# A transformer block on one core: shared exponentials and a new queue order in attention, and PSUM copies on ACT one tile ahead in the output projection

## The chip, the core and the metric

The kernel runs on one core of a Trainium2 chip. The metric is the device time in microseconds (us), lower is better. A core has a matmul engine (PE, TensorE; its weight loads are shown as PEld), a vector engine (DVE), an activation engine (ACT), a general engine (POOL) and a queue processor (SP) that starts DMAs. In these kernels each engine works through its own queue of instructions and waits for the others at semaphores. Every matmul here writes to PSUM, which the kernels use as eight banks of 512 float32 columns, and DVE or ACT takes the results from there, mostly to SBUF.

## The reference

One pre-norm block, batch 1, 2048 tokens, width 1024, bfloat16:

```python
h  = x + A(layernorm(x))      # 32 heads of 32, four segments of 512 tokens
h2 = h + B(layernorm(h))      # SwiGLU, hidden width 3584
# A, for every head and segment s:
p = softmax(q_s @ k_s.T * scale + causal_mask)
o = g * (phi(q_s) @ M) / (phi(q_s) @ z) + (1 - g) * (p @ v_s)   # memory read
M, z = M + phi(k_s).T @ v_s, z + phi(k_s).sum()                 # memory update
# phi(t) = t + 1 where t > 0, exp(t) elsewhere; then o @ wo
```

## The kernel before

The stages follow one another: LN1 with the Q, K, V projections, attention, the output projection with LN2, the feed-forward network (FFN). Attention works on groups `g` of four heads. One segment of one group has four score blocks `kc` (128 keys each; the causal mask leaves 512, 384, 256 and 128 queries). A block's scores for the four heads lie in PSUM banks 0 to 3, and one exp takes all four to SBUF. Because there is one such set of banks, the next block's score matmuls wait for that exp. The triangle on the diagonal is masked afterwards by a multiplication on DVE.

The loop runs the head of segment c together with the tail of the segment before it:

```python
for g in range(NG):                    # 8 groups
    for s in range(NSEG):              # 4 segments
        c = seg_begin(g, s)
        head_kc(c, 0)                  # score matmuls, exp on ACT, mask on DVE
        if prev is not None:
            tail_u_tile(prev, 0)       # exp(scores) @ V, query tile 0; the first
            tail_u_tile(prev, 1)       #   of these waits for the last combine
        head_kc(c, 1)
        if prev is not None:
            tail_u_tile(prev, 2)
        head_kc(c, 2)
        if prev is not None:
            tail_u_tile(prev, 3)
            tail_T(prev)               # transposes of phi(K), copied by DVE
        head_kc(c, 3)
        if prev is not None:
            tail_rest(prev)            # memory read (PE), memory update matmuls (PE),
                                       # combine (DVE: reciprocal, product, sum),
                                       # memory update (DVE: 1 + 8 small operations)
        if s == 1 and g + 1 < NG:
            group_prep(g + 1)          # phi(K), phi(Q) of the next group:
        prev = c                       #   DVE min, ACT exp, DVE max and add; twice
```

The output stage, for 16 tiles of 128 tokens (cut to its order):

```python
t_otT(0); mmA(0)
for t in range(1, NT):
    t_otT(t)        # PE transposes the attention output into banks 0, 1;
                    # DVE copies one half to SBUF, ACT the other
    hadd_ln(t - 1)  # DVE: residual add, LN2 statistics, square root on ACT, apply: hn
    mmA(t)          # 16 matmuls, wait for both copies of t_otT(t)
    ...
    hnT_tr(t - 1)   # PE transposes hn; ACT copies one half, DVE the other
```

The softmax here doesn't subtract the row's maximum and nothing guards it: scores larger than these inputs give would overflow.

## Time and profile before

The median is 1248.84 us of 4 runs (1247.97 to 1251.16). The stage boundaries below are the first transposes of the attention output and the first load of FFN weights.

| stage | from, to (us) | length |
|---|---|---|
| LN1, Q, K, V | 0 to 217 | 217 |
| attention | 217 to 542.9 | 325.9 |
| output projection, LN2 | 542.9 to 642.7 | 99.8 |
| FFN | 642.7 to 1247.2 | 604.5 |

The windows table of the kernel before, for attention and the output stage; its columns are stretch, length, busy time with count for PE, PEld, DVE, ACT and POOL, granted PE clock (1 is full speed), DMA share and GB/s:

```profile
217.00:542.86 325.86, 136.04 (x2656) 82.06 (x2657) 204.08 (x490) 183.34 (x145) 0.00 (x0) 0.51 0.02 8
542.86:642.66 99.80, 77.45 (x512) 39.30 (x512) 69.41 (x144) 25.09 (x49) 0.00 (x0) 0.96 0.15 43
```

Of the 325.9 us of attention, PE is busy 136, DVE 204 and ACT 183. With no engine near full, it is the order of waits that sets the time. The Trainium skill, "Perfetto Trace Analysis", Roofline, says that where matmul and HBM utilization are both low the kernel is bound by latency, that is by stalls and dependencies. The 8 GB/s and 42% PE in this row agree. The granted clock is 0.51.

The timeline of ACT over one group (kernel before; start, length, engine, line, operation, and in brackets the idle time before it with what ended it) shows the rhythm. Line 589 is the exp of a score block, line 552 an exp of the preparation:

```profile
329.17 1.88 ACT L589 ACTIVATE eTbuf<-psall 128x2048 bf16<-128x2048 f32 x1
...
336.62 1.88 ACT L589 ACTIVATE eTbuf<-psall 128x2048 bf16<-128x2048 f32 x1 [0.98 <-PE psall L580]
...
344.63 1.88 ACT L589 ACTIVATE eTbuf<-psall 128x2048 bf16<-128x2048 f32 x1 [0.98 <-PE psall L580]
...
352.39 1.88 ACT L589 ACTIVATE eTbuf<-psall 128x2048 bf16<-128x2048 f32 x1 [0.72 <-PE psall L580]
355.64 1.45 ACT L589 ACTIVATE eTbuf<-psall 128x1536 bf16<-128x1536 f32 x1 [1.38 <-PE psall L580]
357.60 1.02 ACT L589 ACTIVATE eTbuf<-psall 128x1024 bf16<-128x1024 f32 x1 [0.51 <-PE psall L580]
359.03 0.60 ACT L589 ACTIVATE eTbuf<-psall 128x512 bf16<-128x512 f32 x1 [0.40 <-PE psall L580]
363.64 1.48 ACT L552 ACTIVATE tmp<-tmp 128x1536 bf16<-128x1536 bf16 x1 [4.01 <-DVE tmp L548]
367.54 1.48 ACT L552 ACTIVATE tmp<-tmp 128x1536 bf16<-128x1536 bf16 x1 [2.42 <-DVE tmp L548]
369.11 1.88 ACT L589 ACTIVATE eTbuf<-psall 128x2048 bf16<-128x2048 f32 x1
```

The large exps (2048 elements per partition) start 7.45, 8.01, 7.76 and 16.72 us apart: 39.9 us per group. The long one contains the preparation. There the next large exp stands in ACT's queue behind two preparation exps that wait for DVE.

The chain of waits (kernel before; start, length, what) shows why an ordinary segment takes 8 us with 4.95 us of exps:

```profile
344.27 0.37 DVE rrs L709
344.66 1.24 DVE prod L712
345.92 0.70 DVE onat L718
...
346.67 0.52 PE psall L625 x12
347.19 0.47 PE psall L580 x4
347.68 1.46 ACT eTbuf L589
```

The combine (lines 709, 712 and 718) must end before the first twelve attention x V matmuls (line 625) may write to its banks, and the score matmuls of block 1 (line 580) stand behind those in PE's queue. Two groups from the page of the kernel before, the attention x V matmuls and the output projection (line, engine, operation, operands, shapes, count, then busy us and mean ns of one, then the idle time before them and what ended it):

```profile
L625 PE MATMUL psall<-vaug,eTbuf 128*128 128x33 bf16 x1280 | 53.5, 193 | 55.4 <-DVE onat L718 50.1
L849 PE MATMUL psall<-wosb,otT 128*128 128x512 bf16 x256 | 59.4, 386 | 16.0 <-ACT otT L833 16.0
```

PE waits 50.1 us for the combine in attention, and in the output stage 16.0 us for ACT's copy. The timeline of one tile there (kernel before):

```profile
580.04 3.61 PE L849 MATMUL psall<-wosb,otT 128*128 128x512 bf16 x16 [1.02 <-ACT otT L833]
583.08 0.55 DVE L883 TENSOR_SCALAR hn<-hnat,ln2mv,ln2rstd 128x1024 bf16<-128x1024 bf16 x1
583.68 0.62 PE L896 MATMUL psall<-ident,hn 128*128 128x128 bf16 x8
584.14 0.61 PE L819 MATMUL psall<-ident,onat 128*128 128x128 bf16 x8
585.77 3.61 PE L849 MATMUL psall<-wosb,otT 128*128 128x512 bf16 x16 [1.02 <-ACT otT L833]
```

The projection's matmuls (line 849) start 5.73 us apart (580.04, 585.77), with 1.02 us of PE idle in each tile. Line 883 applies LN2 and gives hn, line 896 is its transposes, line 819 those of the attention output.

### The profile page before, as it was taken

The numbers are of one execution on the slowest core, as the hardware profiler recorded it, in microseconds if no ns is written. First come the engines' busy times: TensorE is split into PE (matmuls) and PEld (weight loads), VectorE is DVE, ScalarE is ACT, GpSimd is POOL, SyncE is SP. The second block draws the span as 40 slices with busy tenths as digits, with TensorE's granted clock in tenths as the row PEclk, the third lists the DMA queues.
The fourth block names the chain that finished last, engine by engine and source line by source line (L and its number), as shares of the span: only waits on it lengthen the run. The fifth ranks groups of instructions, "written<-read, shape, count | busy, mean of one in ns | idle before, by whom it ended". The sixth has DMA issues, their size and how long they took to land.

```text
span 1247.2 us, 16150 instructions
## 1 busy us (share of the span) xinstructions
PE 984.3 (79%) x6752; PEld 470.6 (38%) x6752; DVE 506.8 (41%) x1010; ACT 339.9 (27%) x423; POOL 21.0 (2%) x43
## 2 busy tenths in 40 slices
PE   4988988254334443567859999999999997999997
PEld 2444444132222222334424444444444443444443
DVE  5240310466666665657744333333333331011011
ACT  3224123565555655622221111111111110000000
POOL 1000000000000000000000000000000000011011
PEclk9989999555555555579979999999999998999999
DMA  8000000100000000011121111111211102455453
GB/s 303 1 34 1 1 1 7 62 2 1 1 1 1 1 1 1 1 35 43 51 76 34 35 34 35 34 34 34 63 40 35 34 1 101 142 196 176 161 178 126
DMA packets 54232, 66.05 MB, mean 53 GB/s; under 512 B 1936, under 2 KB 30608, under 8 KB 54160
## 3 DMA queue, kind: packets, MB, share of 16 engines
q1 hardware_dynamic: 52624, 60.83, 15.7%
q0 software_dynamic: 1536, 4.20, 0.9%
q8 instruction: 53, 0.87, 0.3%
q14 instruction: 19, 0.16, 0.0%
HBM read 60.83 MB, written 4.19 MB: 52 GB/s over the span
## 4 chain that ended last, share of the span: by engine, by line
PE 68%; DVE 14%; ACT 14%; issue 2%; DMA 1%; POOL 0%; DVEq 0%; SPq 0%; ACTq 0%; POOLq 0%
PE psall L986 16%; PE psall L992 16%; PE psall L1073 15%; PE psall L383 12%; ACT eTbuf L589 8%; PE psall L849 4%; PE psall L580 3%; DVE prod L712 2%; ACT tmp L552 2%; DVE eTbuf L597 2%; ACT xnT L352 1%; DVE lnst L317 1%; DVE onat L718 1%; DVE pkTg L555 1%; PE psall L625 1%
## 5 line engine op out<-in xcount | busy, mean ns | idle before, releaser
L986 PE MATMUL psall<-hnT,w1b 128*128 128x512 bf16 x896 | 213.3, 381 | 6.6 <-DMA w3b<-in_B_w_dram 6.6
L992 PE MATMUL psall<-hnT,w3b 128*128 128x512 bf16 x896 | 212.8, 381 | 0.0
L1073 PE MATMUL psall<-w2b,hmT 128*128 128x512 bf16 x896 | 196.0, 382 | 7.0 <-DMA w2b<-in_B_w_dram 7.0
L589 ACT ACTIVATE eTbuf<-psall 128x2048 bf16<-128x2048 f32 (+3 forms) x128 | 158.3, 1237 | 84.8 <-PE psall L580 84.1
L1008 DVE TENSOR_TENSOR sg<-sg,psall 128x512 bf16<-128x512 bf16 x112 | 77.0, 688 | 239.7 <-PE psall L992 239.7
L580 PE MATMUL psall<-qT,kT 32*128 32x256 bf16 (+3 forms) x512 | 57.7, 441 | 125.8 <-ACT eTbuf L589 117.9
L1003 ACT ACTIVATE sg<-psall 128x512 bf16<-128x512 f32 x112 | 66.9, 597 | 316.8 <-PE psall L986 316.7
L1073 PEld LDWEIGHTS psall<-w2b,hmT 128*128 128x128 bf16 x896 | 88.1, 98 | 114.8 <-issue 10.8
L986 PEld LDWEIGHTS psall<-hnT,w1b 128*128 128x128 bf16 x896 | 87.9, 98 | 113.3 <-issue 8.6
L992 PEld LDWEIGHTS psall<-hnT,w3b 128*128 128x128 bf16 x896 | 88.0, 98 | 106.9 <-issue 2.2
L625 PE MATMUL psall<-vaug,eTbuf 128*128 128x33 bf16 x1280 | 53.5, 193 | 55.4 <-DVE onat L718 50.1
L1095 DVE TENSOR_TENSOR ob<-hnat,psall 128x512 bf16<-128x512 bf16 x32 | 22.0, 688 | 180.3 <-PE psall L1073 179.9
L597 DVE TENSOR_TENSOR eTbuf<-eTbuf,triu 128x512 bf16<-128x512 bf16 x128 | 54.4, 425 | 81.5 <-ACT eTbuf L589 76.6
L1013 DVE TENSOR_TENSOR hmT<-sg,psall 128x512 bf16<-128x512 bf16 x112 | 76.9, 686 | 3.9
L625 PEld LDWEIGHTS psall<-vaug,eTbuf 128*128 128x128 bf16 x1280 | 43.4, 107 | 88.1 <-DVE onat L718 61.2
L849 PE MATMUL psall<-wosb,otT 128*128 128x512 bf16 x256 | 59.4, 386 | 16.0 <-ACT otT L833 16.0
L383 PE MATMUL psall<-xnT,wq 128*128 128x512 bf16 x256 | 64.1, 415 | 9.0 <-ACT xnT L352 6.8
L580 PEld LDWEIGHTS psall<-qT,kT 32*128 32x128 bf16 x512 | 13.9, 99 | 141.5 <-ACT eTbuf L589 135.5
L383 PE MATMUL psall<-xnT,wk 128*128 128x512 bf16 x256 | 55.9, 379 | 0.0
L383 PE MATMUL psall<-wv,xnT 128*128 128x512 bf16 x256 | 55.9, 379 | 0.0
L383 PEld LDWEIGHTS psall<-xnT,wq 128*128 128x128 bf16 x256 | 26.3, 105 | 45.6 <-issue 10.4
L392 DVE CAST qT<-psall 128x512 bf16<-128x512 f32 x32 | 21.3, 687 | 53.2 <-PE psall L383 53.2
(70 smaller groups left out, 594.0 us busy)
## 6 DMA issues: line engine op xcount, KB each, us to landing
w2b<-in_B_w_dram SPq DMA_DIRECT2D x28, 1024.0 KB, 5.3
w1b<-in_B_w_dram SPq DMA_DIRECT2D x14, 512.0 KB, 4.0
w3b<-in_B_w_dram SPq DMA_DIRECT2D x14, 512.0 KB, 5.3
xb<-in_A_x_dram SPq DMA_DIRECT2D x4, 1024.0 KB, 7.0
xr<-in_A_x_dram SPq DMA_DIRECT2D x16, 256.0 KB, 2.7
out_dram<-ob POOLq DMA_DIRECT2D x32, 128.0 KB, 2.4
wq<-in_A_wq_dram SPq DMA_DIRECT2D x1, 2048.0 KB, 13.0
wk<-in_A_wk_dram SPq DMA_DIRECT2D x1, 2048.0 KB, 17.8
```

The costliest lines, as they stand in the source:

```text
L383: o = pe.matmul(self.bank(b), lhsT, rhs, start=(c == 0), stop=(c == NKC - 1))
L580: o = pe.matmul(self.bank(j, N), lhsT, rhs, start=True, stop=True, tile_position=(32 * j, 0))
L589: o = act.activation(eTbuf[:, :, offs[kc]:offs[kc] + N], src, AF.Exp, scale=scale)
L597: o = dve.tensor_tensor(eTbuf[:, :, offs[kc]:offs[kc] + 128], eTbuf[:, :, offs[kc]:offs[kc] + 128], self.triu[:, :].unsqueeze(1).to_broadc ...
L625: o = pe.matmul(self.ps_all[:, ucol(j, i):ucol(j, i) + 33], lhsT, rhs, start=(kc == 0), stop=(kc == i))
L849: o = pe.matmul(self.bank(bb + half), ob[:, c, :], self.wo_sb[:, c, half * 512:(half + 1) * 512], start=(c == 0), stop=(c == NKC - 1))
L986: o = pe.matmul(self.bank(bg), w1b[i][:, c, jj * 128:(jj + 1) * 128], self.hnT[:, c, tc * 512:(tc + 1) * 512], start=(c == 0), stop=(c == ...
L992: o = pe.matmul(self.bank(bu), w3b[i][:, c, jj * 128:(jj + 1) * 128], self.hnT[:, c, tc * 512:(tc + 1) * 512], start=(c == 0), stop=(c == ...
L1003: o = act.activation(sg[si][:, :], self.bank(bg), AF.Sigmoid)
L1008: o = dve.tensor_tensor(sg[si][:, :], sg[si][:, :], self.bank(bg), op=ALU.mult)
L1013: o = dve.tensor_tensor(self.hmT[:, fc, tc * 512:(tc + 1) * 512], sg[si][:, :], self.bank(bu), op=ALU.mult)
L1073: o = pe.matmul(self.bank(bb), self.hmT[:, fc, t * 128:(t + 1) * 128], w2b[k % 2][:, jj, half * 512:(half + 1) * 512], start=(fc == 0), st ...
```

## The change

The intent in attention is to take the round trips and the combine out of PE's way: blocks 1 and 3 (384 + 128 columns) share one exp, only one attention x V tile stands before them, the rest of the tail goes behind them, and the masks go behind the combine. In the output stage the intent is to have the copied transposes ready before they are wanted. The diff, cut to its core:

```diff
+            offs = [0, 512, 1024, 896]
...
-            def head_kc(c, kc):
+            def head_kc(c, kc, emit_mask=True):
+                blocks = [(1, 0), (3, 384)] if kc == 1 else [(kc, 0)]
+                N = 512 if kc == 1 else L - 128 * kc
...              # matmuls of both blocks into one set of banks, then one exp of N columns
+                if emit_mask:
+                    emit_mask_kc(c, kc)
...              # tail_rest is cut in two: tail_nd_combine and tail_M
                     head_kc(c, 0)
                     if prev is not None:
                         tail_u_tile(prev, 0)
+                    head_kc(c, 1, emit_mask=False)
+                    if prev is not None:
+                        tail_T(prev)
                         tail_u_tile(prev, 1)
-                    head_kc(c, 1)
+                        tail_u_tile(prev, 2)
+                        tail_u_tile(prev, 3)
+                        tail_nd_combine(prev)      # memory read, combine
+                    head_kc(c, 2, emit_mask=False)
+                    prep = s == 1 and g + 1 < NG
+                    if not prep:
+                        for kc in (1, 2, 3):
+                            emit_mask_kc(c, kc)
                     if prev is not None:
-                        tail_u_tile(prev, 2)
-                    head_kc(c, 2)
-                    ...
-                        tail_rest(prev)
-                    if s == 1 and g + 1 < NG:
+                        tail_M(prev)               # memory update
+                    if prep:
                         group_prep(g + 1)
+                        for kc in (1, 2, 3):
+                            emit_mask_kc(c, kc)
...
# output stage
-                o = dve.tensor_copy(ob[:, 0:4, :], ...)            # otT, first half
+                o = act.activation(ob[:, 0:4, :], ..., AF.Copy)
-                o = dve.tensor_copy(self.hnT[:, 4:8, ...], ...)    # hnT, second half
+                o = act.activation(self.hnT[:, 4:8, ...], ..., AF.Copy)
             t_otT(0)
+            t_otT(1)
             mmA(0)
             for t in range(1, NT):
-                t_otT(t)
+                if t + 1 < NT:
+                    t_otT(t + 1)
```

More of the change, by code (lines that the diff above doesn't have):

```diff
@@ L470, in phase_C @@
             o = 0
-            for kc in range(QT):
-                offs.append(o)
-                o += (L - 128 * kc)
+            offs = [0, 512, 1024, 896]
             eTbufs = [self.sb(es, f"eTbuf{i}", [128, 4, NTOT], BF16, side="left")
@@ L568, in seg_begin @@
                             t_mask={})
-            def head_kc(c, kc):
+            def head_kc(c, kc, emit_mask=True):
                 g, seg0, ebi, eTbuf = c["g"], c["seg0"], c["ebi"], c["eTbuf"]
                 t_exp, t_mask = c["t_exp"], c["t_mask"]
-                N = L - 128 * kc
+                blocks = [(1, 0), (3, 384)] if kc == 1 else [(kc, 0)]
+                N = 512 if kc == 1 else L - 128 * kc
                 for j in range(4):
@@ L576, in head_kc @@
                 vp = None
-                for j in range(4):
-                    lhsT = self.kT[32 * j:32 * j + 32, g, seg0 + 128 * kc: seg0 + 128 * kc + 128]
-                    rhs = self.qT[32 * j:32 * j + 32, g, seg0 + 128 * kc: seg0 + L]
-                    o = pe.matmul(self.bank(j, N), lhsT, rhs, start=True,
-                                  stop=True, tile_position=(32 * j, 0))
-                    if j == 3:
-                        vp = S_.mark("pe", o)
+                for kb, coff in blocks:
+                    Nb = L - 128 * kb
+                    for j in range(4):
+                        lhsT = self.kT[32 * j:32 * j + 32, g, seg0 + 128 * kb: seg0 + 128 * kb + 128]
+                        rhs = self.qT[32 * j:32 * j + 32, g, seg0 + 128 * kb: seg0 + L]
+                        o = pe.matmul(self.bank(j, Nb, off=coff), lhsT, rhs, start=True,
+                                      stop=True, tile_position=(32 * j, 0))
+                        if j == 3:
+                            vp = S_.mark("pe", o)
                 S_.wait("act", vp)
@@ L590, in head_kc, with emit_mask_kc @@
                 ve = S_.mark("act", o)
-                t_exp[kc] = ve
+                for kb, coff in blocks:
+                    t_exp[kb] = ve
                 for j in range(4):
                     bank_read[j] = ve
-                S_.wait("dve", ve)
+                if emit_mask:
+                    emit_mask_kc(c, kc)
+            def emit_mask_kc(c, kc):
+                eTbuf = c["eTbuf"]
+                t_exp, t_mask = c["t_exp"], c["t_mask"]
+                S_.wait("dve", t_exp[kc])
                 S_.wait("dve", tk["triu"])
@@ L657, in tail_T, with tail_nd_combine @@
                 c["t_pkcopy"] = vcp
-            def tail_rest(c):
+            def tail_nd_combine(c):
                 g, s, seg0, ebi = c["g"], c["s"], c["seg0"], c["ebi"]
@@ L675, in tail_rest @@
                     v_last = v_nd
-                if s < NSEG - 1:
-                    S_.wait("pe", c["t_pkcopy"])
-                    vM = None
-                    moff = MB * 512 + 256
-                    for j in range(4):
-                        h = 4 * g + j
-                        for kc in range(QT):
-                            lhsT = pk_nat[:, kc, 32 * j:32 * j + 32]
-                            rhs = self.vaug[:, s * QT + kc, h, 0:33]
-                            o = pe.matmul(self.ps_all[32 * j:32 * j + 32, moff:moff + 33],
-                                          lhsT, rhs, start=(kc == 0), stop=(kc == QT - 1),
-                                          tile_position=(0, 32 * j))
-                            if j == 3 and kc == QT - 1:
-                                vM = S_.mark("pe", o)
-                    st["t_pk_read"] = vM
                 S_.wait("dve", v_last)
@@ L725, in tail_rest @@
                 bank_read[6] = vd
-                if s < NSEG - 1:
-                    S_.wait("dve", st["t_pk_read"])
-                    S_.wait("dve", S_.cur("dve"))
-                    if s == 0:
-                        o = dve.tensor_copy(self.Mf[:, :], self.bank(MB, 33, off=256))
-                    else:
-                        o = dve.tensor_tensor(self.Mf[:, :], self.Mf[:, :],
-                                              self.bank(MB, 33, off=256), op=ALU.add)
-                    vdm = S_.mark("dve", o)
-                    S_.wait("dve", vdm)
-                    S_.wait("dve", t_gcol)
-                    S_.wait("dve", tk["msb0"])
-                    for j in range(4):
-                        o = dve.tensor_scalar(self.Msb[32 * j:32 * j + 32, j, 0:32],
-                                              self.Mf[32 * j:32 * j + 32, 0:32],
-                                              gcol4[32 * j:32 * j + 32, g:g + 1], None, op0=ALU.mult)
-                        S_.mark("dve", o)
-                        o = dve.tensor_scalar(self.Msb[32 * j:32 * j + 32, j, 32:33],
-                                              self.Mf[32 * j:32 * j + 32, 32:33],
-                                              omgcol4[32 * j:32 * j + 32, g:g + 1], None, op0=ALU.mult)
-                        st["t_M_dve"] = S_.mark("dve", o)
-                    bank_read[MB] = vdm
@@ new lines, in tail_M @@
+            def tail_M(c):
+                g, s = c["g"], c["s"]
+                if s >= NSEG - 1:
+                    return
+                S_.wait("pe", c["t_pkcopy"])
+                vM = None
+                moff = MB * 512 + 256
+                for j in range(4):
+                    h = 4 * g + j
+                    for kc in range(QT):
+                        lhsT = pk_nat[:, kc, 32 * j:32 * j + 32]
+                        rhs = self.vaug[:, s * QT + kc, h, 0:33]
+                        o = pe.matmul(self.ps_all[32 * j:32 * j + 32, moff:moff + 33],
+                                      lhsT, rhs, start=(kc == 0), stop=(kc == QT - 1),
+                                      tile_position=(0, 32 * j))
+                        if j == 3 and kc == QT - 1:
+                            vM = S_.mark("pe", o)
+                st["t_pk_read"] = vM
+                S_.wait("dve", vM)
+                S_.wait("dve", S_.cur("dve"))
+                if s == 0:
+                    o = dve.tensor_copy(self.Mf[:, :], self.bank(MB, 33, off=256))
+                else:
+                    o = dve.tensor_tensor(self.Mf[:, :], self.Mf[:, :],
+                                          self.bank(MB, 33, off=256), op=ALU.add)
+                vdm = S_.mark("dve", o)
+                S_.wait("dve", vdm)
+                S_.wait("dve", t_gcol)
+                S_.wait("dve", tk["msb0"])
+                for j in range(4):
+                    o = dve.tensor_scalar(self.Msb[32 * j:32 * j + 32, j, 0:32],
+                                          self.Mf[32 * j:32 * j + 32, 0:32],
+                                          gcol4[32 * j:32 * j + 32, g:g + 1], None, op0=ALU.mult)
+                    S_.mark("dve", o)
+                    o = dve.tensor_scalar(self.Msb[32 * j:32 * j + 32, j, 32:33],
+                                          self.Mf[32 * j:32 * j + 32, 32:33],
+                                          omgcol4[32 * j:32 * j + 32, g:g + 1], None, op0=ALU.mult)
+                    st["t_M_dve"] = S_.mark("dve", o)
+                bank_read[MB] = vdm
@@ L756, in phase_C @@
                         tail_u_tile(prev, 0)
+                    head_kc(c, 1, emit_mask=False)
+                    if prev is not None:
+                        tail_T(prev)
                         tail_u_tile(prev, 1)
-                    head_kc(c, 1)
-                    if prev is not None:
-                        tail_u_tile(prev, 2)
-                    head_kc(c, 2)
-                    if prev is not None:
-                        tail_u_tile(prev, 3)
-                        tail_T(prev)
-                    head_kc(c, 3)
-                    if prev is not None:
-                        tail_rest(prev)
-                    if s == 1 and g + 1 < NG:
+                        tail_u_tile(prev, 2)
[6 more added lines that the diff above has]
+                            emit_mask_kc(c, kc)
+                    if prev is not None:
+                        tail_M(prev)
+                    if prep:
                         group_prep(g + 1)
+                        for kc in (1, 2, 3):
+                            emit_mask_kc(c, kc)
                     prev = c
@@ L773, in phase_C @@
             tail_T(prev)
-            tail_rest(prev)
+            tail_nd_combine(prev)
+            tail_M(prev)
             self.t_attn_done_dve = S_.cur("dve")
@@ L823, in t_otT @@
                 if t - 2 in t_mmA:
-                    S_.wait("dve", t_mmA[t - 2])
                     S_.wait("act", t_mmA[t - 2])
-                S_.wait("dve", vT)
-                S_.wait("dve", S_.cur("dve"))
-                o = dve.tensor_copy(ob[:, 0:4, :],
-                                    self.bank_bf(0)[:, 0:512].rearrange("p (k n) -> p k n", k=4))
-                vc0 = S_.mark("dve", o)
                 S_.wait("act", vT)
                 S_.wait("act", S_.cur("act"))
+                o = act.activation(ob[:, 0:4, :],
+                                   self.bank_bf(0)[:, 0:512].rearrange("p (k n) -> p k n", k=4),
+                                   AF.Copy)
+                vc0 = S_.mark("act", o)
                 o = act.activation(ob[:, 4:8, :],
@@ L906, in hnT_tr @@
                 vcpa = S_.mark("act", o)
-                S_.wait("dve", vT)
-                S_.wait("dve", S_.cur("dve"))
-                o = dve.tensor_copy(
+                o = act.activation(
                     self.hnT[:, 4:8, t * 128:(t + 1) * 128],
-                    self.bank_bf(7)[:, 0:512].rearrange("p (k n) -> p k n", k=4))
-                vcpd = S_.mark("dve", o)
+                    self.bank_bf(7)[:, 0:512].rearrange("p (k n) -> p k n", k=4), AF.Copy)
+                vcpd = S_.mark("act", o)
                 t_hnTcopy[t] = (vcpa, vcpd)
```

## The prediction

> **What bounds it now.** Stages by the table of windows: LN1+QKV 0-217 us, attention 217-543, output projection+LN2 543-643, FFN 643-1247 (matmul-bound, clock 0.97-0.99, untouched by the diff). In attention no engine is full (of 326 us: PE 136, DVE 204, ACT 183, clock 0.51); it is a latency loop. The timeline repeats every 39.95 us per group of four segments: exponential-to-exponential starts are 7.45, 8.01, 7.76 and, around the next group's preparation, 16.72 us. A segment runs score matmuls -> exp on ACT -> score matmuls into the same four banks, four times: exps 1.88+1.45+1.02+0.60 = 4.95, ACT gaps 0.72-1.18, 0.61, 0.51, 0.40. On top, the chain of waits crosses to DVE: mask, copy of phi(K), mask, reciprocal, product, sum, and only then (PE idle 2.1 us) the first attention x V matmuls, which stand ahead of the next score matmuls in PE's queue. The output stage takes 5.73 us per tile: PE waits 1.02 us each time for the ACT copy of the transposed attention output; that is 16.0 us in the table of groups.
>
> **What changes.**
> 1. Score blocks 1 and 3 share one exp of 4x512: 32 fewer exps (19.1 us out, 32x(1.88-1.45) = 13.7 us in) and one fewer round trip, about 0.4 us of gap, per segment.
> 2. Only tile 0 of attention x V stands before the packed scores; tiles 1-3, the transposes and the memory-read matmuls go behind them, under a 1.88 us exp (measured issue rate 28 ns each: 36 = 1.0, 16 = 0.45, transposes 0.45; total about 1.9: just fits). The combine (2.4 us of DVE) then starts right after and ends before the next segment's tile 0 needs it.
> 3. Masks 1-3 move behind the combine; in the preparation segment behind the preparation. DVE busy time does not change.
> 4. Output stage: both PSUM copies go to ACT (0.60 instead of 0.43 each), and transposes run one tile ahead, so the copy hides under 3.6 us of matmuls.
>
> **Sums (estimates from these durations).** Ordinary segment: exps 4.78 + gaps 0.72+0.76 (eight matmuls)+0.51 = 6.8 us. DVE needs about 6.45 of that, so it fits barely. Preparation segment: exp0 to the memory update's end 7.1, then min 0.6, exp 1.5, phi(K) 1.8, min 0.6, exp 1.5: 13.2 us (now 16.7), because combine and memory update are done earlier. Group: 33.6 against 39.95; seven such groups save 44, the last about 3: attention -47 us. Output stage: 4.6-4.7 us per tile; -15 us after a longer start. Almost all of it is on the critical path, since the stages are serial.
>
> **Prediction: 1187 us, 80% range 1174 to 1206. Faster by over 2%: 0.96; within 2%: 0.035; slower: 0.005.**
>
> **What would show it.** Attention window about 279 us; 96 exps instead of 128, with ACT busy down about 5 us; segment starts 6.8 us apart, 13.2 around preparation; the PE wait on the combine gone from the longest waits; output stage 80-85 us with no PE wait on the otT copy; FFN unchanged.
>
> **What would make it wrong.** PE missing the 1.9 us slot, or DVE, with 0.3 us to spare per segment, becoming the loop: each 0.3 us per segment costs about 10 us. LN2's square root queued behind four ACT copies could delay the hn transposes. Upside: the clock. The Trainium skill, "TensorE: Matmul & The Clock Gate", Part 1, says PE stays at 4/8 until a busy window of about 3.4 us; the trace agrees (0.50 throughout attention, PE busy 42%). I assume it stays there at about 49% busy; full clock would save more.

## The result and the profile after

The changed kernel takes 1177.57 us (median of 8 runs, 1174.99 to 1179.72) against 1248.88 us (13 runs); the ratio is 0.9424, 95% interval 0.9415 to 0.9434, that is 71 us less. The outputs are correct.

| stage | before | after | difference | predicted |
|---|---|---|---|---|
| LN1, Q, K, V | 217 | 217 | 0 | 0 |
| attention | 325.9 | 276.1 | -49.7 | -47 |
| output projection, LN2 | 99.8 | 80.1 | -19.7 | -15 |
| FFN | 604.5 | 602.9 | -1.7 | 0 |

I do not count the 1.7 us of the FFN as the change's: over the traces of kernels with the same FFN its length lay between 602.7 and 606.0 us.

The windows of the changed kernel for the same two stages:

```profile
217.00:493.14 276.14, 125.11 (x2656) 79.79 (x2657) 204.11 (x490) 177.89 (x113) 0.00 (x0) 0.52 0.03 9
493.14:573.21 80.07, 73.13 (x512) 40.18 (x512) 55.83 (x112) 40.73 (x81) 0.00 (x0) 0.95 0.18 54
```

DVE's busy time in attention is what it was (204 us) and ACT's is 5 us less; the stage became 50 us shorter all the same. The mean granted clock is still about half (0.52).

The timeline of ACT over one group (changed kernel; line 590 is the score exp, line 550 the preparation's):

```profile
299.58 1.88 ACT L590 ACTIVATE eTbuf<-psall 128x2048 bf16<-128x2048 f32 x1 [0.72 <-PE psall L581]
302.18 1.88 ACT L590 ACTIVATE eTbuf<-psall 128x2048 bf16<-128x2048 f32 x1 [0.72 <-PE psall L581]
304.56 1.02 ACT L590 ACTIVATE eTbuf<-psall 128x1024 bf16<-128x1024 f32 x1 [0.51 <-PE psall L581]
...
311.15 1.48 ACT L550 ACTIVATE tmp<-tmp 128x1536 bf16<-128x1536 bf16 x1 [2.42 <-DVE tmp L546]
312.72 1.88 ACT L590 ACTIVATE eTbuf<-psall 128x2048 bf16<-128x2048 f32 x1
...
319.45 1.88 ACT L590 ACTIVATE eTbuf<-psall 128x2048 bf16<-128x2048 f32 x1 [0.72 <-PE psall L581]
...
326.18 1.88 ACT L590 ACTIVATE eTbuf<-psall 128x2048 bf16<-128x2048 f32 x1 [0.72 <-PE psall L581]
...
332.92 1.88 ACT L590 ACTIVATE eTbuf<-psall 128x2048 bf16<-128x2048 f32 x1 [0.72 <-PE psall L581]
```

The first exps of the segments now start 13.14 us apart around the preparation and then 6.73, 6.73 and 6.74 us: 33.3 us per group. The slot under the packed exp in one segment, PE and ACT alone, from the timeline of the changed kernel:

```profile
321.93 0.61 PE L650 MATMUL psall<-ident,pkTg 128*128 128x128 bf16 x4
322.05 1.88 ACT L590 ACTIVATE eTbuf<-psall 128x2048 bf16<-128x2048 f32 x1 [0.72 <-PE psall L581]
322.33 1.23 PE L633 MATMUL psall<-vaug,eTbuf 128*128 128x33 bf16 x36
323.39 0.61 PE L679 MATMUL psall<-Msb,pqTg 128*128 128x33 bf16 x16
323.98 0.40 PE L581 MATMUL psall<-qT,kT 32*128 32x256 bf16 x4
```

Most of what PE does for the older segment (transposes line 650, the 36 attention x V matmuls of tiles 1 to 3 line 633, memory read line 679) is started between 321.93 and 323.98, beside the exp that runs from 322.05 to 323.93. Only the four matmuls of tile 0 stand before it and those of the memory update after the next scores. The next score matmuls start 0.05 us after that exp, no later than after the exp before it (which ended at 321.33; scores at 321.38). The work just fits.

The groups of the changed kernel that answer to those of before, and the output stage's timeline:

```profile
L633 PE MATMUL psall<-vaug,eTbuf 128*128 128x33 bf16 x1280 | 48.9, 193 | 11.3 <-DVE onat L711 10.8
L864 PE MATMUL psall<-wosb,otT 128*128 128x512 bf16 x256 | 59.7, 388 | 0.0
```

```profile
511.25 3.62 PE L864 MATMUL psall<-wosb,otT 128*128 128x512 bf16 x16
514.71 0.61 PE L911 MATMUL psall<-ident,hn 128*128 128x128 bf16 x8
515.15 0.61 PE L836 MATMUL psall<-ident,onat 128*128 128x128 bf16 x8
515.60 3.62 PE L864 MATMUL psall<-wosb,otT 128*128 128x512 bf16 x16
```

PE's wait for the combine fell from 50.1 us to 10.8 us (line 633 against 625), and its wait in front of the projection from 16.0 us to nothing (line 864 against 849). Its matmuls now start 4.35 us apart (511.25, 515.60).

### The profile page after: what moved, and what is told of

Read it like the earlier page. It is cut to its first block, busy times and chain, and to the rows that moved or that the text cites. A ratio compares the mean times of both kernels' runs of the same rounds, so it can differ in the third digit from the quotient of the medians.

```text
span 1176.1 us, 16031 instructions
## 1 busy us (share of the span) xinstructions
PE 964.4 (82%) x6752; PEld 468.1 (40%) x6752; DVE 493.1 (42%) x978; ACT 350.0 (30%) x423; POOL 21.0 (2%) x43
## 3 DMA queue, kind: packets, MB, share of 16 engines
q0 software_dynamic: 1536, 4.20, 1.0%
## 4 chain that ended last, share of the span: by engine, by line
PE 73%; ACT 12%; DVE 11%; issue 2%; DMA 1%; POOL 0%; DVEq 0%; SPq 0%; ACTq 0%; POOLq 0%
PE psall L1001 17%; PE psall L1007 16%; PE psall L1088 16%; PE psall L383 13%; ACT eTbuf L590 8%; PE psall L864 4%; PE psall L581 3%; ACT tmp L550 2%; ACT xnT L352 1%; DVE lnst L317 1%; DVE pkTg L553 1%; DVE Msb L750 1%; PE psall L633 1%; DVE eTbuf L605 1%; DVE prod L705 1%
## 5 line engine op out<-in xcount | busy, mean ns | idle before, releaser
L590 ACT ACTIVATE eTbuf<-psall 128x2048 bf16<-128x2048 f32 (+1 forms) x96 | 152.9, 1593 | 57.3 <-PE psall L581 56.5
L581 PE MATMUL psall<-qT,kT 32*128 32x128 bf16 (+3 forms) x512 | 50.9, 440 | 135.9 <-ACT eTbuf L590 131.8
L383 PE MATMUL psall<-xnT,wq 128*128 128x512 bf16 x256 | 61.3, 402 | 11.8 <-ACT xnT L352 6.8
L581 PEld LDWEIGHTS psall<-qT,kT 32*128 32x128 bf16 x512 | 11.2, 102 | 147.8 <-ACT eTbuf L590 142.5
L633 PE MATMUL psall<-vaug,eTbuf 128*128 128x33 bf16 x1280 | 48.9, 193 | 11.3 <-DVE onat L711 10.8
## 6 DMA issues: line engine op xcount, KB each, us to landing
wq<-in_A_wq_dram SPq DMA_DIRECT2D x1, 2048.0 KB, 13.1
```

The lines of the kernel that those rows point to most:

```text
L383: o = pe.matmul(self.bank(b), lhsT, rhs, start=(c == 0), stop=(c == NKC - 1))
L581: o = pe.matmul(self.bank(j, Nb, off=coff), lhsT, rhs, start=True, stop=True, tile_position=(32 * j, 0))
L590: o = act.activation(eTbuf[:, :, offs[kc]:offs[kc] + N], src, AF.Exp, scale=scale)
L633: o = pe.matmul(self.ps_all[:, ucol(j, i):ucol(j, i) + 33], lhsT, rhs, start=(kc == 0), stop=(kc == i))
```

## The experiments

All kernels gave correct results, and each was timed in three rounds against the kernel before. Medians are of 4 runs. Where two experiments are compared with each other, the ratio of each to the kernel before is used. "Attention" and "output stage" in what was measured are the stages of the table above, read from each run's trace.

### The two stages apart

**e1_attn_only**: the kernel before, with the attention part of the diff alone.

```diff
 # before + attention part of the change; the output stage stays:
 t_otT(0); mmA(0)      # copies on DVE and ACT, no tile ahead
```

> The kernel before with the attention part of the change alone. Theory (the two stages are serial, so their gains add): attention about 278 us instead of 326, output stage unchanged at 5.73 us per tile; total about 1200 us (1198 to 1202), ratio 0.961. Rival (part of the shorter output stage comes from what attention leaves behind, for instance a warmer PE clock at its start): output stage already under 95 us here, total under 1196 us.

Measured: 1197.76 us, ratio 0.9598 (0.9573 to 0.9624). Attention ended at 492.8 us and the output stage took 100.2 us. The warmer-clock rival is out: the output stage does not profit from what attention leaves behind.

**e2_out_only**: the kernel before, with the output-stage part alone.

```diff
 # before + output part of the change; attention stays:
 head_kc(c, 0); tail_u_tile(prev, 0); tail_u_tile(prev, 1); head_kc(c, 1); ...
```

> The kernel before with the output-projection part of the change alone (copies on ACT and transposes one tile ahead). Theory: 4.35 us per tile as in the changed kernel, total about 1227 us (1226 to 1229), ratio 0.983, the same 21 us that the two traces differ by in that stage. Rival, my prediction's term: only the 1.02 us wait goes, 4.7 us per tile, total about 1233 us.

Measured: 1227.67 us, ratio 0.9825 (0.9808 to 0.9842), output stage 80.3 us. The gain is 21 us, and my prediction's term of 15 us is refuted. The two parts together make 51 + 21 = 72 us against 71 measured for the whole: they add.

### The output stage taken apart

**e3_ahead_only**

```diff
 # before, with the transposes one tile ahead; the four copies stay on DVE and ACT
             t_otT(0)
+            t_otT(1)
             mmA(0)
             for t in range(1, NT):
-                t_otT(t)
+                if t + 1 < NT:
+                    t_otT(t + 1)
```

> The kernel before with the transposes one tile ahead, but the PSUM copies shared by DVE and ACT as before. Theory: DVE becomes the loop, because the copy of hnT stands in its queue behind a round trip over PE (otT copy 0.49 + LN2 chain 3.96 + wait for the transposes 0.72 + hnT copy 0.45 = about 5.6 us per tile against 5.73): total 1246 to 1249 us, no verdict of faster. Rival (running ahead removes PE's wait, so it earns the gain alone): 4.4 to 4.8 us per tile, total 1228 to 1234 us.

Measured: 1248.74 us, ratio 1.0003 (0.9978 to 1.0028): the same. PE's wait in front of the projection is gone (0.6 us in all), and nothing was gained. The timeline of this run shows where the time went (line 883 applies LN2 and gives hn, line 896 is its transposes, 909 and 828 are DVE's two copies, 863 the next tile's residual add):

```profile
597.56 0.55 DVE L883 TENSOR_SCALAR hn<-hnat,ln2mv,ln2rstd 128x1024 bf16<-128x1024 bf16 x1
598.17 0.62 PE L896 MATMUL psall<-ident,hn 128*128 128x128 bf16 x8 [1.21 <-DVE hn L883]
598.83 0.42 DVE L909 COPY hnT<-psall 128x512 bf16<-128x512 bf16 x1 [0.71 <-PE psall L896]
599.35 0.42 DVE L828 COPY otT<-psall 128x512 bf16<-128x512 bf16 x1
599.88 1.29 DVE L863 TENSOR_TENSOR hnat<-xr,psall 128x512 bf16<-128x512 bf16 x2
```

DVE finishes hn, sits 0.71 us until PE's transposes are done, makes two copies, and only then begins the next tile's residual add. Its next hn comes at 603.30, 5.74 us after this one: the rhythm of the kernel before. The Trainium skill, "TensorE: Matmul & The Clock Gate", says in the table at its head that the queues of ScalarE and VectorE are strict first-in, first-out. The trace agrees: the add's projection had ended before PE began the transposes at 598.17, yet the add started at 599.88, behind the copies.

**e4_copies_only**

```diff
 # before, with all copies on ACT; no tile ahead
-                o = dve.tensor_copy(ob[:, 0:4, :], ...)
+                o = act.activation(ob[:, 0:4, :], ..., AF.Copy)
-                o = dve.tensor_copy(self.hnT[:, 4:8, ...], ...)
+                o = act.activation(self.hnT[:, 4:8, ...], ..., AF.Copy)
```

> The kernel before with all four PSUM copies of the output stage on ACT, without running ahead. Theory: the otT copies queue on ACT behind the two hnT copies, so PE's wait before the projection grows from 1.0 to about 2 us; about 6.3 us per tile, total 1255 to 1260 us. Rival (it is the relief of DVE's LN2 chain that matters): faster than before by 3 us or more.

Measured: 1265.24 us, ratio 1.0131 (1.0111 to 1.0152): 16 us slower, in the direction of the theory and 5 us outside its range. In steady state a tile takes 6.50 us and PE waits 2.0 us for the copies. That is 12 us over 16 tiles. For the rest there is one observation: the projection matmuls averaged 423 ns here against 388 ns in e1 and e2, and the granted clock of the stage was 0.90 against 0.96 in the kernel before. I made no run that separates this.

So each half of the output change alone is worth nothing or costs 16 us, and both together gain 21 us. The wait was held by two queues in turn: opening one hands it to the other.

**e12_hnT_dve**, made last, asks which copy matters.

```diff
 # the changed kernel, with one copy given back to DVE
-                o = act.activation(self.hnT[:, 4:8, ...], ..., AF.Copy)
+                S_.wait("dve", vT)
+                o = dve.tensor_copy(self.hnT[:, 4:8, ...], ...)
```

> The changed kernel with only the second hnT copy given back to DVE (the otT copies stay on ACT, transposes stay one tile ahead). Theory, from e3_ahead_only: that copy stands in DVE's queue behind hn -> PE transposes, and the next tile's LN2 behind it, so DVE loops at 3.96 + 0.72 + 0.45 = about 5.15 us per tile instead of 4.35: about 12 us slower than the changed kernel, 1187 to 1192 us. Rival (0.42 us of DVE work matters only as busy time): at most 4 us slower, under 1182 us.

Measured: 1188.69 us, ratio 0.9528 (0.9509 to 0.9547), 11 us slower than the changed kernel, with 5.20 us per tile. One copy of 0.42 us costs 0.85 us per tile because of where it stands: DVE cannot pass it, and it waits for PE, which waits for DVE.

### Attention taken apart

The following keep the new output stage; e2_out_only (ratio 0.9825) is their kernel with the old attention, the changed kernel (0.9424) the one with the new.

**e5_order_only**

```diff
 # the changed kernel, with four separate exps
-            offs = [0, 512, 1024, 896]
+            offs = [0, 512, 896, 1152]
-                blocks = [(1, 0), (3, 384)] if kc == 1 else [(kc, 0)]
+                blocks = [(kc, 0)]
                     head_kc(c, 2, emit_mask=False)
+                    head_kc(c, 3, emit_mask=False)
```

> The changed kernel with four separate exps per segment (the packing undone, the new order and the new output stage kept). Theory: exps 4.95 + gaps 0.72+0.61+0.51+0.40 = 7.2 us per segment, and 0.45 us more where PE's 1.9 us of work no longer fits under the 1.45 us exp of block 1; 13.6 us around the preparation; group 36 us instead of 33.3; total about 1197 us (1192 to 1201). Rival (packing is worth only its 0.17 us of exp time plus nothing else): total 1183 to 1186 us.

Measured: 1202.57 us, ratio 0.9617 (0.9601 to 0.9633), 1.6 us outside the range. Segments take 7.60, 7.59 and 7.19 us, and 14.0 us around the preparation; a group takes 36.4 us (forecast 36). In the full segments the gap before the third exp is 0.9 us instead of 0.5: PE's work does not fit under the shorter exp. PE's wait for the combine is gone here too (0.4 us, 50.1 in the kernel before), so it is the order that removes it.

**e6_pack_only**

```diff
 # the old order of the loop, with blocks 1 and 3 in one exp
+                blocks = [(1, 0), (3, 384)] if kc == 1 else [(kc, 0)]
                     head_kc(c, 2)
                     if prev is not None:
                         tail_u_tile(prev, 3)
                         tail_T(prev)
-                    head_kc(c, 3)
```

> The order of the kernel before in attention, with blocks 1 and 3 in one exp (the reordering undone, packing and the new output stage kept); to be compared with e2_out_only at about 1227. Theory: the first attention x V matmuls still stand before the packed scores and wait for the combine, so the segment stays about 8 us; gain 0 to 10 us, total 1217 to 1227. Rival (parts add: one exp and one round trip fewer is worth 0.5 us in each of 32 segments whatever the order): total about 1211 us or less.

Measured: 1225.79 us, ratio 0.9806 (0.979 to 0.9822). Against e2_out_only that is 0.0019 of the time of before, about 2 us and within the intervals. One exp and one round trip fewer per segment gained nearly nothing in the old order: PE still waited 41.9 us for the combine (50.1 before). There is a second cause, special to this order: with block 3 gone, no exp lies between the transposes of phi(K) and the memory update matmuls that need their copy, and PE's wait for that copy grew from 5.5 to 20.1 us. A group shows both, gain and loss: one of its segments is 1.0 us shorter (6.76 us, 7.76 before), another 0.5 us longer (7.98, 7.46 before).

Order alone is worth 0.0208 (26 us), packing alone 0.0019 (2 us), both 0.0401 (50 us). The missing 22 us appear only together: packing takes a round trip out of a loop that has become the bound, and it makes the exp long enough to hide PE's work. How much of the 22 us is only the new wait of e6_pack_only, no run separates; packing with another place for the transposes in the old order was not tried.

**e7_masks_first**

```diff
 # the changed kernel; in the preparation segment the masks too go first
-                    if not prep:
-                        for kc in (1, 2, 3):
-                            emit_mask_kc(c, kc)
+                    for kc in (1, 2, 3):
+                        emit_mask_kc(c, kc)
                     if prev is not None:
                         tail_M(prev)
                     if prep:
                         group_prep(g + 1)
-                        for kc in (1, 2, 3):
-                            emit_mask_kc(c, kc)
```

> The changed kernel with the three masks ahead of the memory update and the preparation in the preparation segment too, as in the other segments. Theory: DVE's preparation chain is what the next exp waits for, so 1.35 us of masks in front of it (minus up to 0.2 us of slack) lengthens seven segments: about 8 us, total 1184 to 1187. Rival (the masks fill DVE idle time there, the chain starts no later): 1177 to 1179.

Measured: 1190.58 us, ratio 0.9523 (0.9508 to 0.9537), 13 us slower than the changed kernel where I had expected 8. The timeline of DVE in this run shows the term that I had left out:

```profile
308.83 0.88 DVE L605 TENSOR_TENSOR eTbuf<-eTbuf,triu 128x512 bf16<-128x512 bf16 x2 [0.38 <-ACT eTbuf L590]
309.82 0.19 DVE L741 COPY Mf<-psall 128x33 f32<-128x33 f32 x1
```

Two of the masks wait 0.38 us for the last exp, and the memory update and the preparation stand behind them. So each preparation segment grows by 1.73 us (14.87 against 13.14), that is 1.35 of masks and 0.38 of waiting; seven times that is 12 us. The position of three masks in DVE's queue is worth as much as a quarter of attention's gain.

**e8_msb_one**

```diff
 # the changed kernel; eight small multiplications become one
-                for j in range(4):
-                    o = dve.tensor_scalar(self.Msb[32*j:32*j+32, j, 0:32], ..., gcol4[...])
-                    o = dve.tensor_scalar(self.Msb[32*j:32*j+32, j, 32:33], ..., omgcol4[...])
+                o = dve.tensor_tensor(self.Msb, self.Mf (broadcast over j), GM[:, g], op=ALU.mult)
# GM: block-diagonal table of the gates for all groups, built once
```

> The changed kernel with the eight small multiplications of each memory update (1.52 us) done as one on a precomputed gate table. Theory (ordinary segments are bound by the exp-score loop, only the preparation chain by DVE): seven preparation segments 1.2 us shorter, about 3 us more set-up at the start of attention; 5 to 8 us faster, 1169 to 1173 us. Rival (DVE is the loop of ordinary segments too, being busy 6.5 of 6.7 us): 24 updates times 1.2 us, about 25 us faster, 1150 to 1155 us.

Measured: 1171.02 us, ratio 0.9371 (0.9356 to 0.9385), 6.6 us faster than the changed kernel. The segments around the preparation went from 13.14 to 11.91 us, the ordinary ones stayed at 6.72 or 6.73. DVE is not the loop of ordinary segments, though it is busy most of the time; its work is dear only where ACT waits for it. About 29 us of DVE work gone (24 times 1.52 less 0.30) gave 6.6 us, after a set-up that keeps PE waiting 2.8 us longer at the start of attention (6.4 against 3.6).

### What the experiments point to

The 13.1 us segment around the preparation is the largest remaining loss.

**e9_prep_spread**

```diff
 # the changed kernel, preparation spread over three segments
-                        group_prep(g + 1)
+                    # s == 1: the two minimums (DVE)
+                    # ACT: six exps of 512 columns; after head_kc(c, 0) and after
+                    #      head_kc(c, 2) of s = 2, s = 3 and s = 0 of the next group
+                    # DVE: phi(K) at the end of s = 0, phi(Q) at the end of s = 1
```

> The changed kernel with the preparation of the next group taken out of one segment: its two minimum operations stay there, its exps are cut into six of 512 columns that stand in the 0.72 us gaps of ACT in the next three segments, its two outputs follow on DVE a segment later. Theory: the 13.1 us segment becomes an ordinary one; the group is then bound by DVE, which has 26.9 us of work per group, so 27 to 28.5 us per group instead of 33.3: 34 to 42 us faster, 1136 to 1144 us. Rival (DVE work in queue order makes new waits, for DVE is full): over 29.5 us per group, 1151 us or more.

Measured: 1153.79 us, ratio 0.9226 (0.9207 to 0.9244). This is 24 us faster than the changed kernel, not 34 to 42; it falls where the rival had put it. A group takes 30.0 us (segments of 9.53, 6.72, 6.72 and 7.07 us). In the trace the first exp piece waits 2.80 us for DVE's minimum, in front of the next large exp, in six of the seven preparations (0.80 us in the first). That wait is the whole excess of the 9.53 us segment over the ordinary ones.

**e10_spread_msb**: e9_prep_spread with e8_msb_one's single multiplication (the diffs of both).

> e9_prep_spread and e8_msb_one together. Theory: DVE then needs 23.2 us per group and the exp-score loop is the bound again at 6.75 us per segment, 27.0 us per group: 0 to 8 us faster than e9_prep_spread, 1130 to 1140 us. Rival (DVE was not the bound in e9_prep_spread): slower than e9_prep_spread by the 3 us of set-up.

Measured: 1145.52 us, ratio 0.9166 (0.915 to 0.9181), 8 us faster than e9_prep_spread but 5.5 us over the absolute range. A group takes 28.7 us (8.31, 6.72, 6.73 and 6.93), so the 27.0 us of the theory was not reached. The same wait is still there, shorter, as the timeline of ACT of this run shows:

```profile
299.87 0.63 ACT L591 ACTIVATE tmp<-tmp 128x512 bf16<-128x512 bf16 x1 [1.58 <-DVE tmp L584]
300.59 1.88 ACT L636 ACTIVATE eTbuf<-psall 128x2048 bf16<-128x2048 f32 x1
```

**e11_spread_later**

```diff
 # e10_spread_msb, each exp piece one gap later
-                    if s == 2 and more: prep_exp(g + 1, "k", 0)     # after head_kc(c, 0)
+                    if s == 2 and more: prep_exp(g + 1, "k", 0)     # after head_kc(c, 2)
# and so on for the other five
```

> e10_spread_msb with each of the six exp pieces one gap later. In e10_spread_msb a group takes 28.6 us, and ACT waits 1.58 us per group with the first piece for the minimum on DVE, in front of the next exp. Theory: this wait goes and nothing comes in its place; 27.0 us per group, about 11 us faster than e10_spread_msb, 1132 to 1137 us. Rival (DVE is late at that point anyway and holds up the next exp in another way): under 4 us gained, over 1141 us.

Measured: 1137.55 us, ratio 0.9111 (0.9097 to 0.9126), 8 us faster than e10_spread_msb and just above the range. A group takes 27.3 us. This version beats both kernels: it is 111 us faster than the kernel before and 40 us faster than the changed one, with correct results. That a move by one gap, with no work taken away, gains 8 us shows that in e10_spread_msb the wait came from the place of the pieces and not from the amount of work. The same move was not tried on e9_prep_spread itself, so how much of its longer wait was DVE's fullness stays open.

## Why the prediction was right, and where its sizes were off

- **The bound in attention: right.** The loop of waits, not an engine's busy time, set the stage. DVE's busy time did not change (204.08 and 204.11 us in the stage's windows of the two traces) while the stage lost 50 us, and e8_msb_one took away 29 us of DVE work (24 us with its set-up counted) for 6.6 us.
- **Ordinary segment 6.8 us, preparation segment 13.2 us, group 33.6 us: right.** Measured 6.73, 13.14 and 33.3. The 0.3 us per group make up most of the difference between the 49.7 us that attention lost and the 47 predicted. DVE did not become the loop, as the prediction had feared (e8_msb_one): it is busy 5.9 us of an ordinary segment of 6.73, not counting the short gaps between its instructions.
- **"PE ... just fits": right.** It fits under the 1.88 us exp and not under the 1.45 us one of e5_order_only. The prediction listed packing and order as separate items; e5_order_only and e6_pack_only show that they are not separate. That did not spoil the sum, because the sum was made for the loop with both.
- **Masks behind the preparation: right, and worth more than the text lets one see** (12 to 13 us, e7_masks_first).
- **The clock stays at half: right, but for two short releases.** Its mean was 0.52 in attention after the change, at 45% PE busy. The Trainium skill, "TensorE: Matmul & The Clock Gate", Part 1, says that the clock is released after a busy window, and the trace agrees: full speed was granted twice, from 285.12 to 288.54 and from 418.24 to 421.66 us. In the 3.41 us before each of the two, PE was busy 3.05 and 3.11 us. It gained next to nothing: the three segments there took 6.51, 6.63 and 6.88 us instead of 6.73 each.
- **The output stage, "4.6-4.7 us per tile; -15 us": the mechanism right, the size too small.** The tile takes 4.35 us, the stage lost 19.7 us. The term was made by taking the 1.02 us of PE idle out of 5.73 us. More went with it than that. From the start of the transposes of the attention output to the start of the projection the traces show 1.63 us before (584.14 to 585.77) and 0.45 us after (515.15 to 515.60), 1.18 us less: with the 1.02 us of idle also goes 0.16 us at the end of the transposes, which the profile books as busy (PE's ends are modelled in it). And from the start of the projection to the transposes of hn it is 3.64 us before (580.04 to 583.68) and 3.46 us after (511.25 to 514.71), because before, hn came only at 583.63, 3.59 us after the start of the projection, and PE waited for it; DVE, which no longer makes the copies, delivers it 3.27 us after (514.52). These are 0.16 and 0.18 us per tile over the 1.02, about 5 us over the stage.
- **The worry about "LN2's square root queued behind four ACT copies": no harm seen.** The changed output stage is at PE's own pace but for about 0.2 us of weight loads waiting for hn. The danger in this stage lay on the other engine: with one copy left on DVE it costs 11 us (e12_hnT_dve), and the lookahead alone gains nothing (e3_ahead_only).
- **The sum:** 62 us were predicted and 71 measured. Of the 9 us, about 5 are the output stage, 3 attention, and the rest the FFN's scatter between runs.

## What to carry to other kernels

When a loop goes over several engines, write down for each engine the order of its queue, and add up the loop with durations from the trace; busy shares say little, and a small operation costs what stands behind it in the queue. Two changes that remove different waits of the same loop must be tried together: alone, one of them may gain nothing or even lose, because the other wait takes over. An exp or another long operation is also a slot for other engines, so its length should match the work that is to hide under it.

## What the Trainium skill lacked or had wrong

- "TensorE: Matmul & The Clock Gate", Part 1, names a busy window of about 3.4 us but not how busy it must be. Here PE was 42% busy (before), 45% (after) and 53% (e11_spread_later: 125.0 of 234 us) in attention, and the mean granted clock was 0.51 to 0.52 in all three. The changed kernel was granted full speed for 3.41 us after stretches of that length with PE busy 3.05 and 3.11 us, but not after one with 3.02 us (254.40 to 257.82), nor was the kernel before after one with 3.09 us (261.32 to 264.73). These figures give no sharp limit.
- The same page, Part 4, gives about 275 ns for a transpose in a kernel and says that the full clock does not engage for transposes. Here the 128x128 transposes of a group start 56 ns apart (median) in the output stage (clock 0.95 to 0.96) and 106 ns apart in attention (clock 0.5), so between matmuls that keep the clock up they do run at the higher clock. Whether transposes alone would release it, no run shows.
- "ScalarE: Activation LUTs", What ACT_TABLE_LOAD costs, gives 186 ns + 0.833 ns per column for an ACTIVATE with immediate scale and bias. The exps here, from PSUM, took 597, 1024, 1451 and 1877 ns for 512, 1024, 1536 and 2048 columns: the same slope, with 171 ns instead of 186. From SBUF to SBUF, the preparation's exps of 1536 columns took 1482 ns, which leaves 202 ns. The page has one figure for both.
- No page gives the round trip ACT to PE to ACT, which set attention's loop, as one figure: ACT was idle 0.72 us when the score matmuls between two exps had 512 columns, 0.51 us with 256 and 0.40 us with 128 (at half clock).
